# Loading q for two chunks at once, with two tokens per partition, and storing twelve token tiles late

## The chip, the cores and the metric

The kernel runs on one core of a Trainium2 chip. The core has a matrix engine (TensorE, PE), a vector engine (VectorE, DVE), a scalar engine (ScalarE, ACT), a general engine (GpSimd, POOL) and a synchronisation engine (SyncE, SP), and 16 DMA engines that move data between the large memory (HBM) and the on-chip memory (SBUF). The metric is the device time of one execution in microseconds (us); lower is better.

## The reference

There are two stages. The first is a gated linear attention, a recurrence over 768 tokens for 4 x 8 heads of width 48. The second takes its output, 3072 tokens of width 384, through two matrix products with a squared relu between them.

```python
def _attn_ref(q, k, v, alpha):            # each (4, 8, 768, 48), float32
    for t in range(S):
        state = alpha[:, :, t, :, None] * state + np.einsum('bhd,bhe->bhde', k[:, :, t], v[:, :, t])
        y[:, :, t] = np.einsum('bhd,bhde->bhe', q[:, :, t], state)

def _moe_ref(x, w_in, w_out):             # x: y as (3072, 384); w_in (384, 2048); w_out (2048, 384)
    r = np.maximum(x @ w_in, 0.0)
    return (r * r) @ w_out                # (3072, 384), float32
```

## The kernel before

**Tiles.** The 3072 tokens are 24 chunks (or token tiles) of 128 tokens; a batch has six. Each chunk goes through the attention in its chunked form: the logarithm of alpha is summed along the chunk by a matmul with a triangular matrix, exponentials of the sums scale q and k, the scores q·k are masked with the triangle `utri_b` (the `sm` multiplies), and the output is the masked scores times v plus q times the state of the chunks before. The result is turned into `xT_big`, which holds x transposed. Then groups of one, two or four tiles go through the second stage: w_in, relu on ScalarE (`r`), square on DVE (`gT`), w_out, eviction into `ob` or `keep`, and a store of 128 rows of 1536 B.

**Two ways for q and k.** Up to chunk 10, q and k are scaled in token order and turned by TensorE. From chunk `RAW` = 11 on they are "raw": POOL casts them to bf16 (`rawb`), SP issues a DMA transpose for each (`rawt`), and DVE multiplies the turned tiles by exponentials that ScalarE makes from turned sums (`e_qAT`, `e_kiT`, lines 507 and 510).

**Loads.** SP issues one load of 192 KB for each of q, k, v and alpha of a chunk (line 371). Its pieces are 192 B long, since a head's 48 numbers of one token are contiguous. Six buffers for each tensor let loads run up to six chunks ahead. SP works in order: a DMA transpose that waits for a POOL cast holds up the loads behind it. The alpha loads (`at`) feed the logarithm on ScalarE (line 396).

**Order.** A planner (`Plan`) lays out all operations by estimated durations before the program is emitted, and every engine then runs its own list in that order. A gate (`LEAD`) keeps the attention a few chunks ahead of the second stage, and the matmuls of both are interleaved on TensorE.

**Stores.** Tiles 0 to 7 (`HELD` = 8) are kept in SBUF and stored by two SP transfers of four tiles each, planned for 150 us on (line 763). Tiles 8 to 17 are written out as they come: 5 to 17 are given to POOL (`POOL_OUT`), so that POOL issues ten stores (line 772). Tiles 18 to 22 are issued by SP (line 772), and tile 23 by SP in two halves of 192 columns (line 721). `ob` has six buffers. The chunks 18 to 22 are turned into `xT_big` by DMA transposes from SP (line 620), the others by TensorE.

Of the kernel before, what the change touches and what calls it, by code (L numbers as in the profile page):

```python
# [38 lines left out]
class Op:  # L39


    def __init__(self, eng, dur, emit, deps=(), prio=0.0, takes=None, gives=None, lat=None, at=0.0):
        self.eng, self.dur, self.emit = eng, dur, emit
        self.deps = []
        for d in deps:
            if d is not None:
                d = d if isinstance(d, tuple) else (d, None)
                if d[0] is not None:
                    self.deps.append(d)
        self.prio = prio  # L50
        self.takes, self.gives, self.lat, self.at = takes, gives, lat, at
        self.start = self.done = None

# [5 lines left out]
class Plan:  # L59
# [13 lines left out]
    def ready(self, op):  # L73
        t = op.at
        slack = PE_SLACK if "PE" in op.durs else 0.0
        if slack and self.free.get("PE", 0.0) > PE_CALM:
            slack = 0.25
        for d, x in op.deps:
            if d.done is None:
                return None  # L80
            if x is None:
                t = max(t, d.done + (slack if d.eng != "PE" else 0.0))
            else:
                t = max(t, d.start + d.dur + x)
        if op.takes is not None:
            best = None
            for sl in op.takes:
                f = sl.free_at()
                if f is not None and (best is None or f < best):
                    best, op.slot = f, sl  # L90
            if best is None:
                return None
            t = max(t, best)
        return t

    def run(self, gate):
        free = self.free
        while any(self.pending.values()):
# [34 lines left out]
            if op.takes is not None:  # L133
                self.ready(op)
                op.slot.release.append(op.gives if op.gives is not None else op)
            self.order.append(op)
            self.on_pick(op)
# [4 lines left out]
def kernel(  # L142
# [26 lines left out]
    w_out_r = moe_w_out.rearrange("(j p) n -> p j n", p=P)  # L169
    out_r = out.rearrange("(tt p) n -> tt p n", p=P)  # L170

    consts = ctx.enter_context(tc.tile_pool(name="consts", bufs=1))
# [24 lines left out]
    utri_b = consts.tile([P, 1, P], BF16)  # L197
    nc.gpsimd.tensor_copy(utri_b[:, 0, :], utri_f)
    JN, JP = 4, 32
    JW = P + JN - 1  # L200
# [29 lines left out]
    nc.vector.memset(ae_s, 0.0)  # L230
    xT_big = big.tile([P, KT, n_tok], BF16)
    gT_s = big.tile([P, FT, 2 * P], BF16, name="gT2", tag="gT2")
# [78 lines left out]
    EARLY = 4  # L311
    RAW = 11
    XTURN = (18, 23)
    TLD, TLAT, TLATE = 1.0, 4.0, 2.0
    NR = 3
    R = {}

    def raw_tiles():
        if R:
            return  # L320
        R["b"] = stage.tile([P, NR, 2, H, DP], BF16, name="rawb", tag="stage")
        nc.gpsimd.memset(R["b"][:, :, :, :, D:], 0.0)
        R["t"] = stage.tile([P, NR, 2, NP, P], BF16, name="rawt", tag="stage")
        R["i"] = stage.tile([P, 2, NP, P], BF16, name="aiT", tag="stage")

# [38 lines left out]
    def add_load(s, nm):  # L364
        d = C[s]
        b, c = divmod(s, NCH)

        def ld():
            if nm not in d:
                d[nm] = loads.tile([P, H, D], FP32, name=nm)  # L370
            pin(nc.sync.dma_start(out=d[nm], in_=SRC[nm][b, c]))
        prev = C[s - LB].get("use_" + nm) if s >= LB else None
        d["ld_" + nm] = add("DMA", LD if s < 4 else LD1, ld, prev, lat=2.0 if s < 4 else LAG if s < 6 else 2.4, at=0.6)

    def add_chunk(s):
        d = C[s]
        b, c = divmod(s, NCH)
# [30 lines left out]
        if raw:  # L408
            w, wz = s % NR, s % 2

            def e_rb(j, nm):
                raw_tiles()
                pin(nc.gpsimd.tensor_copy(R["b"][:, w, j, :, 0:D], d[nm]))  # L413

            def e_turn(j):
                pin(nc.sync.dma_start_transpose(out=R["t"][:, w, j], in_=R["b"][:, w, j].rearrange("p h d -> p (h d)")))
            rt = []
            for j, nm in enumerate(["qt", "kt"]):
                cb = add("POOL", 0.55, lambda j=j, nm=nm: e_rb(j, nm), d["ld_" + nm],
                         *([C[s - NR]["turn"][j]] if s >= RAW + NR else []), prio=-5.0)  # L420
                d["use_" + nm] = cb
                t_ = add("TR", TLD, lambda j=j: e_turn(j), cb, *([C[s - NR]["turned"][j]] if s >= RAW + NR else []), lat=TLAT)
                t_.late = TLATE
                rt.append(t_)
            d["turn"] = rt
        vb = d["use_vt"] = add("POOL", 0.55, e_vb, d["ld_vt"], old, prio=-5.0)
# [22 lines left out]
        def e_AT():  # L449
            d["qkT"] = work.tile([P, 2 * NP, P], BF16, name="qkT")  # L450
            pin(nc.scalar.activation(d["qkT"][:, NP:2 * NP, :], d["pmT"], AF.Exp))  # L451

# [25 lines left out]
        if raw:  # L478
# [9 lines left out]
            aiT = add("ACT", 0.48, e_AiT, pT, after(aT), *([C[s - 2]["turned"][1]] if s >= RAW + 2 else []), **g)  # L488
            pT.gives = aiT
            if not last:  # L490
                ae0 = add("ACT", 0.18, lambda: e_aeT(0), pT, after(aiT), **g)
# [14 lines left out]
        def e_qAT():  # L506
            pin(nc.vector.tensor_mul(d["qkT"][:, 0:NP, :], R["t"][:, w, 0], d["qkT"][:, NP:2 * NP, :]))

        def e_kiT():
            pin(nc.vector.tensor_mul(d["qkT"][:, NP:2 * NP, :], R["t"][:, w, 1], R["i"][:, wz]))  # L510
        if raw:
            if not last:
                mk = d["use_kt"] = add("DVE", 0.47, e_kI, ai, d["ld_kt"], old, **g)
            cp = add("DVE", 0.34, e_qAT, aT, rt[0], **g)
            cpk = add("DVE", 0.34, e_kiT, aiT, rt[1], cp, **g)
            d["turned"] = [cp, cpk]
        else:
            mq = d["use_qt"] = add("DVE", 0.47, e_qA, a_, d["ld_qt"], old, **g)
            mk = d["use_kt"] = add("DVE", 0.47, e_kI, ai, d["ld_kt"], old, **g)

        def e_p1q():
# [26 lines left out]

        def e_p2():
            sc = d["sc"] = ps_sc.tile([P, 2, NP, P], FP32, name="sc")  # L550
            t = d["qkT"]
            for p in range(NP):
                for hh in range(2):
                    sl = slice(64 * hh, 64 * hh + 64)
                    mm(sc[:, hh, p, :], lhsT=t[sl, NP + p, :], rhs=t[sl, p, :], start=True, stop=True)
        p2 = d["p2"] = plan.add(Op("PE", 0.42, e_p2, [cp, cpk], takes=[sl_sc], lat=0.10, **g))

        def e_sm(hh):
            if hh == 0:
                d["sm"] = work.tile([P, 2, NP, P], BF16, name="sm")  # L560
            pin(nc.vector.tensor_mul(d["sm"][:, hh], d["sc"][:, hh], utri_b.to_broadcast([P, NP, P])))  # L561
        sm0 = add("DVE", 0.6, lambda: e_sm(0), p2, **g)
        sm1 = add("DVE", 0.6, lambda: e_sm(1), p2, after(sm0), **g)
        p2.gives = sm1

        if not last:
# [51 lines left out]
        if XTURN[0] <= s < XTURN[1]:  # L618
            def e_xt():
                pin(nc.sync.dma_start_transpose(out=xT_big[:, :, s * P:(s + 1) * P], in_=d["xn"]))  # L620
            d["x"] = add("TR", 0.8, e_xt, xn, lat=TLAT)
# [5 lines left out]
        def e_xT():  # L627
            cast(xT, xT_big[:, :, s * P:(s + 1) * P], d["px"])
        xT = add({"ACT": 0.36, "DVE": 0.27} if s < EARLY else "DVE", 0.27, e_xT, p4, prio=-9.0)
# [13 lines left out]
    POOL_OUT = (5, 18)  # L643
    HELD, HELD_AT = 8, 150.0
    KEEP, held_ev = {}, []
# [6 lines left out]
    def add_moe1(g, f0, before, lo=0, hi=None, per=1):  # L652
        hi = GN[g] if hi is None else hi
        t0, n = (GT[g] + lo) * P, (hi - lo) * P
        w = per * n
# [35 lines left out]
    def add_last(g, tt, before, pools):  # L691
# [3 lines left out]
        for hf in range(2):  # L695
# [24 lines left out]
            def e_out(box=box, cols=cols):  # L720
                pin(nc.sync.dma_start(out=out_r[t][:, cols], in_=box["ob"]))
            add("OUT", 0.35, e_out, ev, at=0.0)
        return op

    def add_moe2(g, tt, before, box, quarters, pools):
# [22 lines left out]
        def e_ev():  # L748
            if held:
                if t % 4 == 0:  # L750
                    KEEP[t // 4] = stage.tile([P, 4, d_model], FP32, name="keep", tag="stage")
                box["ob"] = KEEP[t // 4][:, t % 4, :]
# [8 lines left out]

        def e_held():
            pin(nc.sync.dma_start(out=out_r[t - 3:t + 1].rearrange("t p n -> p t n"), in_=KEEP[t // 4]))
        if held:
            held_ev.append(ev)
            if t % 4 == 3:
                add("OUT", 2.2, e_held, *held_ev[-4:], at=HELD_AT)
            return op

        def e_out():  # L770
            dma = nc.gpsimd if pool_out else nc.sync
            pin(dma.dma_start(out=out_r[GT[g] + tt], in_=box["ob"]))
        pool_out = POOL_OUT[0] <= GT[g] + tt < POOL_OUT[1]
# [59 lines left out]

    LEAD = 3.7

    def gate(op):
        s = getattr(op, "gla", None)
        if s is not None:
            return s <= LEAD + (prog["m1"] + prog["m2"]) / 5.12
        return True  # L840
# [60 lines left out]
```

## Time and profile before

| | |
|---|---|
| Median of 3 runs | 184.71 us (184.20 to 185.06) |
| Time of the profiled execution | 185.07 us |
| Its span, first to last instruction | 183.4 us |
| PE busy | 177.5 us (97%) |
| DVE, ACT, POOL busy | 127.1, 126.5, 39.4 us |
| Hardware DMA queue (SP's) | 119536 packets, 31.83 MB, 80.7% of 16 engines' span |
| Software DMA queue (POOL's) | 640 packets, 1.97 MB, 3.2% |
| 192 KB loads of q, k, v, alpha: issue to landing | 4.0, 3.6, 3.8, 4.0 us (medians) |
| Stores of 192 KB by SP, halves of 96 KB | 1.9, 1.6 us |

Times in the page and in the views count from the first instruction of the span. The slices cut the span into 40 equal parts; a digit is the busy share in tenths. A row of a timeline has the start, the duration, the engine, the line, the operation, its output and inputs and how often it follows itself; in brackets stands the idle time before it and what ended that. A row of waits has the waiting instruction, the one that ended the wait, the total, the number and the longest. The view of DMA has packets, bytes, the share of 16 engines' time in the stretch asked for, and the issues with their time to landing.

### The profile page before, as it was taken

What the parts mean: (1) busy time and instruction counts of PE and PEld (TensorE: products, weight loads), DVE (VectorE), ACT (ScalarE), POOL (GpSimd) and SP (SyncE); (2) the same over time, 40 slices, a digit from 0 to 9 for tenths busy, and PEclk for the clock granted to TensorE, in tenths of its full rate; (3) what the DMA queues carried; (4) which work ended last, traced back from release to release, by engine and by line L of the source; (5) the groups of instructions that cost most, each with busy time, mean ns of one, the idle gap of its engine ahead of it and who ended that gap; (6) DMA issues with size and microseconds to landing.
All of it is one profiled execution on the core that took longest, in us unless ns stands there. A gap on an engine that the chain in (4) does not pass through costs nothing.

```text
span 183.4 us, 4946 instructions
## 1 busy us (share of the span) xinstructions
PE 177.5 (97%) x1908; PEld 130.5 (71%) x1908; DVE 127.1 (69%) x273; ACT 126.5 (69%) x286; POOL 39.4 (21%) x80
## 2 busy tenths in 40 slices
PE   7999999899999999999999998999999999999993
PEld 2577884567769877867768776667766777778663
DVE  1179898684999998778877867748855984744200
ACT  3677799226859996966967859847975895767321
POOL 8221100021131142132223133342323512000000
PEclk9999999999999999999999999999999999999999
DMA  5999999999999999998999599898898898901022
GB/s 168 215 212 252 302 366 321 326 220 204 177 191 201 194 179 173 141 190 161 150 193 202 113 240 186 161 227 162 170 201 182 176 163 194 301 13 43 12 77 86
DMA packets 120200, 34.12 MB, mean 186 GB/s; under 512 B 112400, under 2 KB 118928, under 8 KB 120176
## 3 DMA queue, kind: packets, MB, share of 16 engines
q1 hardware_dynamic: 119536, 31.83, 80.7%
q0 software_dynamic: 640, 1.97, 3.2%
q8 instruction: 15, 0.25, 0.6%
q14 instruction: 9, 0.07, 0.2%
HBM read 25.17 MB, written 4.72 MB: 163 GB/s over the span
## 4 chain that ended last, share of the span: by engine, by line
PE 49%; DMA 2%; ACT 1%; issue 0%; DVE 0%
PE bank L240 45%; DMA at<-in_alpha_dram 2%; PE sc L240 2%; PE st L240 1%; PE bank L243 1%; ACT aiT L454 0%; ACT r L676 0%; ACT ob L758 0%; ACT L_s L396 0%; ACT ob L716 0%; DVE xT_big L388 0%; ACT qkT L451 0%
## 5 line engine op out<-in xcount | busy, mean ns | idle before, releaser
L240 PE MATMUL bank<-xT_big,w_in_b 128*128 128x256 bf16 (+2 forms) x636 | 76.6, 262 | 0.9 <-ACT r L676 0.7
L240 PE MATMUL bank<-w_out_b,gT 128*128 128x384 bf16 (+1 forms) x400 | 71.6, 320 | 0.5 <-DVE w_out_b L296 0.5
L676 ACT ACTIVATE r<-bank 128x512 bf16<-128x512 f32 x96 | 56.6, 606 | 11.3 <-PE bank L240 9.9
L240 PEld LDWEIGHTS <-w_in_b 128*128 128x128 bf16 x636 | 52.7, 98 | 10.6 <-issue 1.5
L240 PEld LDWEIGHTS <-gT 128*128 128x128 bf16 x416 | 37.2, 98 | 18.7 <-DVE w_out_b L296 1.0
L684 DVE TENSOR_TENSOR gT<-r 128x512 bf16<-128x512 bf16 x96 | 41.8, 453 | 10.2 <-ACT r L676 9.0
L561 DVE TENSOR_TENSOR sm<-sc,utri_b 128x512 bf16<-128x512 f32 x48 | 30.8, 684 | 5.9 <-PE sc L240 5.7
L405 POOL CAST vb<-vt 128x384 bf16<-128x384 f32 x24 | 13.6, 569 | 69.1 <-DMA vt<-in_v_dram 55.2
L386 ACT CAST xn<-bank 128x384 bf16<-128x384 f32 x24 | 11.6, 482 | 11.6 <-PE bank L240 11.5
L505 DVE TENSOR_TENSOR kI_s<-kt,Ainv 128x384 bf16<-128x384 f32 x21 | 12.8, 611 | 7.8 <-ACT Ainv L466 7.8
L240 PEld LDWEIGHTS <-qkT 64*128 64x128 bf16 (+1 forms) x272 | 10.7, 95 | 6.4 <-issue 2.4
L586 ACT CAST sb<-st 128x384 bf16<-128x384 f32 x20 | 9.6, 482 | 7.7 <-DVE st L581 7.5
L758 ACT COPY ob<-bank 128x384 f32<-128x384 f32 x14 | 6.7, 480 | 8.0 <-PE bank L240 8.0
L396 ACT ACTIVATE L_s<-at 128x384 bf16<-128x384 f32 x20 | 10.5, 527 | 2.4 <-DMA at<-in_alpha_dram 2.3
L240 PE MATMUL bank<-warm 128*128 128x256 bf16 (+1 forms) x54 | 10.9, 348 | 1.3 <-DVE warm L188 1.3
L502 DVE TENSOR_TENSOR qA_s<-qt,A 128x384 bf16<-128x384 f32 x11 | 6.3, 575 | 8.0 <-ACT A L462 8.0
L413 POOL CAST rawb<-qt 128x384 bf16<-128x384 f32 x13 | 7.4, 570 | 20.3 <-DMA qt<-in_q_dram 20.3
L413 POOL CAST rawb<-kt 128x384 bf16<-128x384 f32 x13 | 7.6, 587 | 19.0 <-DMA kt<-in_k_dram 11.1
L581 DVE TENSOR_TENSOR st<-st,ae_s 128x384 f32<-128x384 f32 x20 | 11.1, 556 | 0.5 <-PE st L240 0.5
L466 ACT ACTIVATE Ainv<-bank 128x384 bf16<-128x384 f32 x21 | 10.5, 501 | 1.1 <-PE bank L240 1.0
L240 PE MATMUL sc<-qkT 64*128 64x128 bf16 x192 | 9.5, 219 | 0.0
L240 PEld LDWEIGHTS <-sm 128*128 128x128 bf16 x192 | 8.1, 96 | 1.7 <-issue 0.2
(64 smaller groups left out, 165.7 us busy)
## 6 DMA issues: line engine op xcount, KB each, us to landing
qt<-in_q_dram SPq DMA_DIRECT2D x24, 192.0 KB, 4.0
kt<-in_k_dram SPq DMA_DIRECT2D x24, 192.0 KB, 3.6
vt<-in_v_dram SPq DMA_DIRECT2D x24, 192.0 KB, 3.8
at<-in_alpha_dram SPq DMA_DIRECT2D x20, 192.0 KB, 4.0
wo<-in_moe_w_out_dram SPq DMA_DIRECT2D x4, 768.0 KB, 8.5
out_dram<-ob POOLq DMA_DIRECT2D x10, 192.0 KB, 3.1
wi<-in_moe_w_in_dram SPq DMA_DIRECT2D x4, 384.0 KB, 5.3
wi<-in_moe_w_in_dram SPq DMA_DIRECT2D x2, 768.0 KB, 8.3
```

Source lines behind the costliest of these rows:

```text
L240: pin(nc.tensor.matmul(*a, **kw))
L386: pin(nc.scalar.copy(out_t, in_t))
L396: pin(nc.scalar.activation(L[:, :, 0:D], d["at"], AF.Ln))
L405: pin(nc.gpsimd.tensor_copy(d["vb"], d["vt"]))
L413: pin(nc.gpsimd.tensor_copy(R["b"][:, w, j, :, 0:D], d[nm]))
L466: pin(nc.scalar.activation(d["Ai"], d["pm"][:, 0:HD].rearrange("p (h d) -> p h d", h=H), AF.Exp, scale=-1.0))
L505: pin(nc.vector.tensor_mul(kI[:, :, 0:D], d["kt"], d["Ai"]))
L561: pin(nc.vector.tensor_mul(d["sm"][:, hh], d["sc"][:, hh], utri_b.to_broadcast([P, NP, P])))
L581: pin(nc.vector.tensor_mul(st4, st4, bcast(ae, D)))
L586: pin(nc.scalar.copy(d["sbt"], d["st"]))
L676: pin(nc.scalar.activation(box["r"][:, 0:w], box["ph"][:, 0:w], AF.Relu))
L684: pin(nc.vector.tensor_mul(gT[g][:, f0:f0 + per, lo * P:lo * P + n], r, r))
```

## The change

**q in pairs.** `RAW` becomes 10. For the raw chunks, an even chunk and the odd one after it share one load of q of 384 KB (`add_q_pair`): partition p takes the tokens 2p and 2p+1 of 256, so that a piece is 384 B. POOL casts it in two operations and SP turns it in two transposes, one for the even and one for the odd tokens. An even chunk's queries are the first 64 partitions of both, an odd chunk's the last 64. So the queries of a chunk stand in the order of 64 even tokens and then 64 odd ones. The exponential `e_AT` writes in that order, the multiply `e_qAT` reads two blocks of 64, and the mask is `utri_q`, its columns in that order. k, v and alpha stay as they were, one load for each chunk. The rows of x and of the result keep that order up to the store, where `rows(t)` puts them back: the destination is two blocks of 64 rows, each with every second row of the output.

**Late stores.** `HELD` becomes 12: tiles 8 to 11 are kept too, in a tile of their own. Tiles 8 and 9 are stored in one transfer, tiles 10 and 11 in one each.

**Space.** `xT_big` keeps 12 chunks instead of 24 and is written around. q has three pair buffers (`q_s`).

**Prepared but not in use.** Scores of two chunks at a time are written (`DUO`), but its bound of 99 leaves all chunks on the old way.

```diff
+    out_q = out.rearrange("(tt i r) n -> tt r i n", i=DP, r=2)
+    def rows(t):
+        return out_q[t] if t >= RAW else out_r[t]
...
+    utri_q = consts.tile([P, 1, P], BF16)
+    nc.gpsimd.tensor_copy(utri_q[:, 0, :].rearrange("p (r i) -> p r i", r=2), utri_f.rearrange("p (i r) -> p r i", r=2))
...
-    xT_big = big.tile([P, KT, n_tok], BF16)
+    XR = 12
+    xT_big = big.tile([P, KT, XR * P], BF16)
+    q_s = big.tile([P, 3, 2 * HD], FP32)
...
-    RAW = 11
+    RAW = 10
...
+    def add_q_pair(s):
+        b, c = divmod(s, NCH)
+        src = q[b, :, c * P:(c + 2) * P, :].rearrange("h (p r) d -> p h (r d)", r=2)
+        Q = q_s[:, s // 2 % 3, :].rearrange("p (h rd) -> p h rd", h=H)
+        w = s // 2 % 2
+        old = [o for x in (s - LB, s - LB + 1) for o in C[x]["use_q"]]
+        d = C[s]
+        ld = d["ld_qt"] = add("DMA", 1.6, lambda: pin(nc.sync.dma_start(out=Q, in_=src)), *old, lat=2.4, at=0.6)
+        def e_rb(r):
+            raw_tiles()
+            pin(nc.gpsimd.tensor_copy(R["qb"][:, w, r, :, 0:D], Q.rearrange("p h (r d) -> p h r d", r=2)[:, :, r, :]))
+        def e_turn(r):
+            pin(nc.sync.dma_start_transpose(out=R["qt"][:, w, r], in_=R["qb"][:, w, r].rearrange("p h d -> p (h d)")))
...
         def e_AT():
             d["qkT"] = work.tile([P, 2 * NP, P], BF16, name="qkT")
-            pin(nc.scalar.activation(d["qkT"][:, NP:2 * NP, :], d["pmT"], AF.Exp))
+            pin(nc.scalar.activation(d["qkT"][:, NP:2 * NP, :].rearrange("p n (r i) -> p n r i", r=2),
+                                     d["pmT"].rearrange("p n (i r) -> p n r i", r=2), AF.Exp))
...
         def e_qAT():
-            pin(nc.vector.tensor_mul(d["qkT"][:, 0:NP, :], R["t"][:, w, 0], d["qkT"][:, NP:2 * NP, :]))
+            t = R["qt"][:, s // 2 % 2, :, :, s % 2 * 64:(s % 2 + 1) * 64].rearrange("p r n i -> p n r i")
+            m = d["qkT"].rearrange("p n (r i) -> p n r i", r=2)
+            pin(nc.vector.tensor_mul(m[:, 0:NP], t, m[:, NP:2 * NP]))
...
-    HELD, HELD_AT = 8, 150.0
+    HELD, HELD_AT = 12, 150.0
...
-                pin(nc.sync.dma_start(out=out_r[t][:, cols], in_=box["ob"]))
+                pin(nc.sync.dma_start(out=rows(t)[..., cols], in_=box["ob"]))
...
-        def e_held():
-            pin(nc.sync.dma_start(out=out_r[t - 3:t + 1].rearrange("t p n -> p t n"), in_=KEEP[t // 4]))
+        def e_held(lo, n):
+            k = KEEP[lo // 4][:, lo % 4:lo % 4 + n, :]
+            dst = rows(lo) if n == 1 else out_r[lo:lo + n].rearrange("t p n -> p t n")
+            pin(nc.sync.dma_start(out=dst, in_=k[:, 0, :] if n == 1 else k))
...
-            pin(dma.dma_start(out=out_r[GT[g] + tt], in_=box["ob"]))
+            pin(dma.dma_start(out=rows(GT[g] + tt), in_=box["ob"]))
```

In the changed kernel the loads of q pairs have line 415, the casts and transposes of q 419 and 422, those of k 517 and 520, the stores of tiles 12 to 22 line 871, the held ones 857, and the halves of tile 23 line 813.

More of the change, by code (lines that the diff above doesn't have):

```diff
@@ L51, in __init__ @@
         self.takes, self.gives, self.lat, self.at = takes, gives, lat, at
+        self.holds = []
         self.start = self.done = None
@@ L93, in ready @@
             t = max(t, best)
+        for sl, _ in op.holds:
+            f = sl.free_at()
+            if f is None:
+                return None
+            t = max(t, f)
         return t
@@ L135, in run @@
                 op.slot.release.append(op.gives if op.gives is not None else op)
+            for sl, user in op.holds:
+                sl.release.append(user)
             self.order.append(op)
@@ L311 @@
     EARLY = 4
-    RAW = 11
+    RAW = 10
     XTURN = (18, 23)
+    DUO = 99
+    tails = []
     TLD, TLAT, TLATE = 1.0, 4.0, 2.0
@@ L320, in raw_tiles @@
             return
[L321 to L324, printed above, removed]
+        b_ = stage.tile([P, 6, H, DP], BF16, name="rawb", tag="stage")
+        t_ = stage.tile([P, 6, NP, P], BF16, name="rawt", tag="stage")
+        i_ = stage.tile([P, 6, NP, P], BF16, name="aiT", tag="stage")
+        R["qb"] = b_[:, 0:4].rearrange("p (w r) h d -> p w r h d", r=2)
+        R["qt"] = t_[:, 0:4].rearrange("p (w r) n t -> p w r n t", r=2)
+        R["i"] = i_[:, 0:2]
+        R["kt"] = [t_[:, 4], t_[:, 5], i_[:, 2]]
+        R["kb"] = [b_[:, 4], b_[:, 5], i_[:, 3].rearrange("p n (a d) -> p (n a) d", a=2)]
+        R["on"] = True
+        nc.gpsimd.memset(b_[:, :, :, D:], 0.0)
+        nc.gpsimd.memset(R["kb"][2][:, :, D:], 0.0)
     JLD = 1.18
@@ L366, in add_load @@
         b, c = divmod(s, NCH)
+        if nm == "qt" and s >= RAW:
+            if s % 2 == 0:
+                add_q_pair(s)
+            d["ld_qt"] = C[s // 2 * 2]["ld_qt"]
+            return
         def ld():
-            if nm not in d:
+            if nm == "qt":
+                d[nm] = q_s[:, s // 2 % 3, s % 2 * HD:(s % 2 + 1) * HD].rearrange("p (h d) -> p h d", h=H)
+            elif nm not in d:
                 d[nm] = loads.tile([P, H, D], FP32, name=nm)
@@ L373, in add_load @@
         d["ld_" + nm] = add("DMA", LD if s < 4 else LD1, ld, prev, lat=2.0 if s < 4 else LAG if s < 6 else 2.4, at=0.6)
-    def add_chunk(s):
+    def add_q_pair(s):
[11 more added lines that the diff above has]
+            pin(nc.sync.dma_start_transpose(out=R["qt"][:, w, r], in_=R["qb"][:, w, r].rearrange("p h d -> p (h d)")))
+        first = s < RAW + 4
+        d["use_q"], d["qturn"] = [], []
+        for r in range(2):
+            cb = add("POOL", 0.55, lambda r=r: e_rb(r), ld, *([] if first else [C[s - 4]["qturn"][r]]), prio=-5.0)
+            t_ = add("TR", TLD, lambda r=r: e_turn(r), cb, *([] if first else [C[x]["turned"][0] for x in (s - 4, s - 3)]), lat=TLAT)
+            t_.late = TLATE
+            d["use_q"].append(cb)
+            d["qturn"].append(t_)
+        C[s + 1]["use_q"], C[s + 1]["qturn"] = d["use_q"], d["qturn"]
@@ new lines, in add_chunk, with add_scores, dst, e_p2 @@
+    def add_chunk(s):
+        tail = add_head(s)
+        if s < DUO:
+            add_scores(s)
+            tail()
+        elif s % 2 == 0:
+            tails.append(tail)
+        else:
+            add_scores(s - 1, s)
+            tails.pop()()
+            tail()
+    def add_scores(*pair):
+        def dst(s):
+            d = C[s]
+            if len(pair) == 2 and s == pair[0]:
+                d["sc"] = [banks[sl.bank].tile([P, NP, P], FP32, name=f"bank{sl.bank}") for sl in GLA_BANKS]
+            else:
+                t = ps_sc.tile([P, 2, NP, P], FP32, name="sc")
+                d["sc"] = [t[:, hh] for hh in range(2)]
+        def e_p2():
+            for s in pair:
+                dst(s)
+                t = C[s]["qkT"]
+                for p in range(NP):
+                    for hh in range(2):
+                        sl = slice(64 * hh, 64 * hh + 64)
+                        mm(C[s]["sc"][hh][:, p, :], lhsT=t[sl, NP + p, :], rhs=t[sl, p, :], start=True, stop=True)
+        mask = utri_q if pair[0] >= RAW else utri_b
+        def e_sm(d, hh):
+            if hh == 0:
+                d["sm"] = work.tile([P, 2, NP, P], BF16, name="sm")
+            pin(nc.vector.tensor_mul(d["sm"][:, hh], d["sc"][hh], mask.to_broadcast([P, NP, P])))
+        g = dict(prio=-10.0 + pair[0] * 0.01)
+        p2 = plan.add(Op("PE", 0.18 + 0.24 * len(pair), e_p2, [o for s in pair for o in C[s]["cps"]], lat=0.10, **g))
+        for s in pair:
+            d = C[s]
+            d["p2"] = p2
+            sm0 = add("DVE", 0.6, lambda d=d: e_sm(d, 0), p2, prio=-10.0 + s * 0.01)
+            sm1 = add("DVE", 0.6, lambda d=d: e_sm(d, 1), p2, after(sm0), prio=-10.0 + s * 0.01)
+            d["sms"] = [sm0, sm1]
+            p2.holds += [(sl_sc, sm1)] if s == pair[-1] else list(zip(GLA_BANKS, [sm0, sm1]))
@@ L376, in add_chunk, with add_head @@
+    def add_head(s):
         d = C[s]
@@ L409, in add_chunk, with e_rb, e_turn @@
             w, wz = s % NR, s % 2
-            def e_rb(j, nm):
+            def e_rb():
                 raw_tiles()
[L413 to L425, printed above, removed]
+                pin(nc.gpsimd.tensor_copy(R["kb"][w][:, :, 0:D], d["kt"]))
+            def e_turn():
+                pin(nc.sync.dma_start_transpose(out=R["kt"][w], in_=R["kb"][w].rearrange("p h d -> p (h d)")))
+            first = s < RAW + NR
+            cb = d["use_kt"] = add("POOL", 0.55, e_rb, d["ld_kt"], *([] if first else [C[s - NR]["turn"]]), prio=-5.0)
+            d["turn"] = add("TR", TLD, e_turn, cb, *([] if first else [C[s - NR]["turned"][1]]), lat=TLAT)
+            d["turn"].late = TLATE
         vb = d["use_vt"] = add("POOL", 0.55, e_vb, d["ld_vt"], old, prio=-5.0)
@@ L489, in add_chunk @@
             pT.gives = aiT
+            ae1 = None
             if not last:
@@ L506, in e_qAT @@
         def e_qAT():
-            pin(nc.vector.tensor_mul(d["qkT"][:, 0:NP, :], R["t"][:, w, 0], d["qkT"][:, NP:2 * NP, :]))
+            t = R["qt"][:, s // 2 % 2, :, :, s % 2 * 64:(s % 2 + 1) * 64].rearrange("p r n i -> p n r i")
+            m = d["qkT"].rearrange("p n (r i) -> p n r i", r=2)
+            pin(nc.vector.tensor_mul(m[:, 0:NP], t, m[:, NP:2 * NP]))
         def e_kiT():
-            pin(nc.vector.tensor_mul(d["qkT"][:, NP:2 * NP, :], R["t"][:, w, 1], R["i"][:, wz]))
+            pin(nc.vector.tensor_mul(d["qkT"][:, NP:2 * NP, :], R["kt"][w], R["i"][:, wz]))
         if raw:
@@ L513, in add_chunk @@
                 mk = d["use_kt"] = add("DVE", 0.47, e_kI, ai, d["ld_kt"], old, **g)
-            cp = add("DVE", 0.34, e_qAT, aT, rt[0], **g)
-            cpk = add("DVE", 0.34, e_kiT, aiT, rt[1], cp, **g)
+            cp = add("DVE", 0.34, e_qAT, aT, *d["qturn"], **g)
+            cpk = add("DVE", 0.34, e_kiT, aiT, d["turn"], cp, **g)
             d["turned"] = [cp, cpk]
         else:
-            mq = d["use_qt"] = add("DVE", 0.47, e_qA, a_, d["ld_qt"], old, **g)
+            mq = add("DVE", 0.47, e_qA, a_, d["ld_qt"], old, **g)
             mk = d["use_kt"] = add("DVE", 0.47, e_kI, ai, d["ld_kt"], old, **g)
+            d["use_qt"], d["use_q"] = mq, [mq]
         def e_p1q():
@@ L547, in add_chunk, with add_tail @@
             p1q.gives = cp
[L549 to L564, printed above, removed]
+        d["cps"] = [cp, cpk]
+        return lambda: add_tail(s, c, last, d, kI, ae, ae1, mk if not last else None, vb, cp, cast, g)
+    def add_tail(s, c, last, d, kI, ae, ae1, mk, vb, cp, cast, g):
+        sm0, sm1 = d["sms"]
         if not last:
@@ L619, in e_xt @@
             def e_xt():
-                pin(nc.sync.dma_start_transpose(out=xT_big[:, :, s * P:(s + 1) * P], in_=d["xn"]))
+                pin(nc.sync.dma_start_transpose(out=xT_big[:, :, s % XR * P:(s % XR + 1) * P], in_=d["xn"]))
             d["x"] = add("TR", 0.8, e_xt, xn, lat=TLAT)
@@ L627, in e_xT @@
         def e_xT():
-            cast(xT, xT_big[:, :, s * P:(s + 1) * P], d["px"])
+            cast(xT, xT_big[:, :, s % XR * P:(s % XR + 1) * P], d["px"])
         xT = add({"ACT": 0.36, "DVE": 0.27} if s < EARLY else "DVE", 0.27, e_xT, p4, prio=-9.0)
@@ L653, in add_moe1 @@
         hi = GN[g] if hi is None else hi
-        t0, n = (GT[g] + lo) * P, (hi - lo) * P
+        t0, n = (GT[g] + lo) % XR * P, (hi - lo) * P
         w = per * n
@@ L750, in e_ev @@
                 if t % 4 == 0:
-                    KEEP[t // 4] = stage.tile([P, 4, d_model], FP32, name="keep", tag="stage")
+                    KEEP[t // 4] = (stage if t < 8 else big).tile([P, 4, d_model], FP32, name="keep" if t < 8 else f"keep{t}", tag="stage" if t < 8 else f"keep{t}")
                 box["ob"] = KEEP[t // 4][:, t % 4, :]
@@ L766, in add_moe2 @@
             if t % 4 == 3:
-                add("OUT", 2.2, e_held, *held_ev[-4:], at=HELD_AT)
+                n = [x for x in (4, 2, 1) if t - 3 + x <= RAW][0] if t - 3 < RAW else 1
+                lo = t - 3
+                while lo <= t:
+                    m = min(n, 4) if lo < RAW else 1
+                    add("OUT", 0.55 * m, lambda lo=lo, m=m: e_held(lo, m), *held_ev[lo:lo + m], at=HELD_AT)
+                    lo += m
             return op
@@ L834 @@
     LEAD = 3.7
+    DUO_LEAD = 3.7, 3.7
     def gate(op):
@@ L838, in gate @@
         if s is not None:
-            return s <= LEAD + (prog["m1"] + prog["m2"]) / 5.12
+            return s <= (LEAD if s < DUO else DUO_LEAD[s % 2]) + (prog["m1"] + prog["m2"]) / 5.12
         return True
```

## The prediction

> **What bounds the kernel now.** I read the head of the page first, then the chain of waits near the end, then the DMA view of two short stretches of the tail, then the DMA view and the waits of the middle.
>
> ```profile
> span 183.4 us, 4946 instructions
> PE 177.5 (97%) x1908; PEld 130.5 (71%) x1908; DVE 127.1 (69%) x273; ACT 126.5 (69%) x286; POOL 39.4 (21%) x80
> PEclk9999999999999999999999999999999999999999
> DMA  5999999999999999998999599898898898901022
> ```
>
> TensorE works 177.5 of 183.4 us at full clock; the loss is 1.3 us in the first 6 us and 2.9 us after its last matmul, neither touched by the change. The DMA row is the second thing to see: full or nearly so until about 160 us, almost empty in the last 20 us.
>
> ```profile
> 169.94 10.56 PE bank L240 x81
> 180.50 0.02 issue
> 180.52 0.32 ACT ob L716
> ```
>
> The chain ends in matmuls, one eviction at 180.52, and a store. So after the last matmul only that one store is exposed. How a store uses the DMA engines is seen where it runs alone, from 168 to 170 us (one 192 KB store) and from 181 to 183 us (the last half store):
>
> ```profile
> DMA packets 144, 0.20 MB, mean 98 GB/s; under 512 B 16, under 2 KB 144, under 8 KB 144
> q1 hardware_dynamic: 144, 0.20, 26.4%
> out_dram<-ob SPq DMA_DIRECT2D x1, 192.0 KB, 1.9
> ...
> DMA packets 144, 0.10 MB, mean 49 GB/s; under 512 B 16, under 2 KB 144, under 8 KB 144
> q1 hardware_dynamic: 144, 0.10, 14.8%
> ```
>
> 128 rows of data and 16 small packets, one for each engine: these stores are dealt over all 16. The full one takes 26.4% of 16 engines over 2 us, 8.45 us of engine time (0.53 us on each); the half 14.8%, 4.74 us. The next lines are of the middle, 120 to 153 us, with seven POOL stores, of which six take nearly all of the software queue's 10.2%:
>
> ```profile
> q0 software_dynamic: 384, 1.18, 10.2%
> ACT L_s L396 <- DMA at<-in_alpha_dram: 1.2, 2, 0.7
> 109.42 0.52 ACT L396 ACTIVATE L_s<-at 128x384 bf16<-128x384 f32 x1 [0.71 <-DMA at<-in_alpha_dram]
> 111.84 0.49 PE L240 MATMUL bank<-xT_big,w_in_b 128*128 128x256 bf16 x3 [0.66 <-ACT r L676]
> ```
>
> Packets of 1.18 MB are six stores: 10.2% of 33 us of 16 engines is 53.9 us, 9.0 us of engine time for each store beside other traffic. The last three lines show the weak place: ScalarE waits for an `at` load, relu behind it is late, and TensorE stands 0.66 us. It is TensorE's only stall over 0.1 us after 60 us.
>
> **The change part by part.** The profiled execution took 185.07 us, 1.67 over its span; the median of the three runs is 184.71, 0.2% lower. Sums are against 185.07.
>
> *Chunk 10 becomes raw.* TensorE loses eight transposes and four one-column matmuls and gains four 128x128 ones. On the chain three transposes take 0.17 us; with the same 0.055 us for the others, the net is about -0.4 us on the path. ScalarE trades one A (0.49) for two exponentials (0.61, 0.63) and DVE a multiply and a copy (0.58, 0.69) for two multiplies (0.46, 0.44): beside TensorE, with over 11 us of idle ahead of the relus. The stride-2 read of PSUM in the exponential of 14 chunks and the split token order in 14 multiplies cost between nothing and twice their time (8.6 and 6.4 us); I take nothing, as element counts are unchanged, and both engines are idle 31% of the span. If that cover were gone, a relu or a score would be late by at most 0.6 us per chunk.
>
> *q in pairs.* From 56 to 66 us 10441 packets, all under 512 B, take 100.7% of 16 engines: 15.4 ns for each 192 B piece. Fourteen loads of 1024 pieces are 13.8 us on every engine. Seven pair loads have as many pieces each, at a price between 15.4 ns and that of the half store's 768 B rows (4.74 us by 128, 37 ns); by bytes about 23, so 10.3 us. Saved 3.5, between 6.9 and -2.8. Two more transposes (of the raw chunk 10) cost about 0.8 us each: what loads leave of the queue's 85.4% between 66 and 153 us, by 512 packets. SP issues seven fewer loads. Of the pair's two casts POOL does the same work as before, but SP has two transposes in a row to wait for; the waits of DVE for a turned tile are ended by ScalarE in every case, never by the transpose, so a microsecond there is covered.
>
> *Four tiles more stored late.* Tiles 8 to 11 leave the middle: four POOL issues and 4 x 0.53 us on every engine. Together the DMA engines have about 4 us less to do before 150 us. TensorE can win from that only its one stall, 0.66 us.
>
> *Stores in token order.* From tile 10 on, the listing of the changed program shows the store's destination as 2x64x384 where before it was 128x384; SBUF's side still has 128 partitions in front. No transfer of the trace has a leading count other than 128, so the cost has to be bounded. If it is still dealt over 16 engines, 0.53 us each. If an engine's share has to be a block of the leading count on both sides, there are only two shares: 64 rows on each of two engines, 8.45/2 = 4.2 us alone, 9.0/2 = 4.5 us in the middle, and 4.74/2 = 2.4 us for a half. I take two, since the leading count is the one thing on which all 16-way transfers of the trace agree. [...]
>
> *The tail with two engines.* SP's stores share one queue; I take it that they land on the same two engines. Behind the transpose of chunk 22, which landed 5.2 us after its issue at 155.12 (160.3), come tiles 8 and 9 on 16 engines (1.1 us, to 161.4), then 10, 11, 18 to 22: seven by 4.2 is 29.4 us, and two halves, 4.7. That fills the two engines without a gap (tile 18 is issued at 159.15, 19 at 167.96, each earlier than the queue reaches it) to 195.5. Before, the half's packets ended at about 182.1 and the span at 183.4; the same 1.3 us gives 196.8, and with 1.67 it is 198.5. TensorE's own end no longer counts; what counts is when the queue starts, and that follows TensorE through chunk 22. No eviction waits for it: six output buffers lie between.
>
> *The middle with two engines.* Tiles 12 to 17 leave by POOL at 123.6, 132.2, 137.6, 139.7, 146.3 and 152.9. On two engines each occupies them for 4.5 us, where it took 0.56 of every one: a load that crosses is late by up to 3.9 us. The transposes have cover, as said. `at` has none: the last one is issued at 132.80, beside the second of these stores, and is read at 136.4, on landing. I put one such delay on the path, 3.9 us; bounds are none and all five stores ahead of 152 us.
>
> Sum: 198.5 - 0.4 - 0.66 + 3.9 = 201.3, rounded 201.
>
> **The rivals.** *Two engines, middle covered.* The 4 us that the DMA engines save arrive before the stores do, and `at` is early enough: 197.4. For it: all four waits of ScalarE for `at` in the span are 2.3 us together, the longest 0.7. Against: 3.9 us is more than all of these. Chance 0.25.
>
> *Every store goes into the load loop.* SP waits in order for casts, so a late load stops the loads behind it: 5 x 3.9 less 4.2 us saved and about 3.4 us that the last turned k lies ready (issue 150.4, landing 3.4 later, read at 157.2), 11.9 us on TensorE: 209.3. For it: the full DMA row. Against: the row has eights after 130 us, so the queue catches up a little between stores. Chance 0.15.
>
> *Other pairs for other stores.* Then nothing queues: the last half starts at about 181.8, takes 2.4, and ends the span 2.1 us later than now; with the middle as forecast 185.1 + 2.1 + 2.8 = 190. Nothing in the trace speaks for it. Chance 0.08.
>
> *Still 16 engines, faster.* The tail is as before, the 0.66 us stall at 111 us and 0.4 us of matmuls go: 184.0, faster by 0.6%. It decides from the point where a store's 64 rows need not stay on one engine, and would be read from 16 small packets per store. Chance 0.10.
>
> **How the numbers follow.** My forecast has 0.42. The range 193 to 209 holds it, the covered middle (down to 4.2 us less, should one late store go out ahead of that transpose) and most of the serial case; outside lie the last two rivals, 0.18, and a little above. A difference of 0.5% is about what can be told here, the three runs being spread over 0.47%. Faster 0.06 and same 0.04 come from the last rival, which lies at that bound; slower 0.90.
>
> **What would show it.** In the changed profile: a store alone with two small packets, landing 4 to 5 us after issue, later ones 10 us and more; the DMA row at 1 in the last slices where all else is 0; the chain ending in a long DMA step behind L813; loads of 6 to 8 us to landing between 124 and 153 us, and ScalarE waiting for `at` by over 3 us. It is wrong if late stores land in 2 us, or if TensorE's last matmul comes before 180 us and the end within 4 us of it.

## The result, and the profile after

The changed kernel took 213.97 us (median of 6 runs, 209.74 to 214.94) against 184.88 us (6 runs, 184.2 to 186.25) for the kernel before. The ratio, 1.140 with a 95% interval of 1.128 to 1.152, counts only the runs within 1.5% of the fastest of their kernel (209.74 and 212.24 us of the change), so the profiled run and the loss of 29 us read from it lie some 3 us above what the ratio says. The profiled execution took 214.03 us, 28.96 more than that of before. It is slower, as forecast, and 5 us past the upper end of the range.

The head of the page comes first: busy times, then TensorE, its granted clock and the DMA engines in 40 slices of 5.3 us.

```profile
span 212.3 us, 4898 instructions
...
PE 181.5 (85%) x1900; PEld 131.9 (62%) x1900; DVE 127.2 (60%) x272; ACT 128.0 (60%) x288; POOL 39.2 (18%) x80
...
PE   7897899999999999999999997595489999999100
...
PEclk9999999999999999999999999579958999999955
DMA  6998999999989688987969695799994697111110
```

There are two places to see. The DMA row ends in five 1s and a 0, the slices after 180 us, and TensorE is done before the last of them. And in the middle, between about 125 and 165 us, TensorE has gaps and its clock falls below full twice, where before it was full throughout. The chain of waits near its end says when TensorE is done:

```profile
145.19 9.67 DMA xT_big<-xn
...
154.90 7.38 PE bank L256 x37
...
178.88 18.29 PE bank L256 x144
197.17 0.02 issue
197.20 0.32 ACT ob L808
```

The last matmul ends at 197.17 us, where it was 180.50: 16.7 us later. From there to the end of the span it is 15.1 us, where it was 2.9: 12.2 us more. Together 28.9 us, the whole loss. So there are two halves to explain. The second is read from the DMA view of 180 to 184 us, where only a store is under way:

```profile
DMA packets 135, 0.20 MB, mean 51 GB/s; under 512 B 3, under 2 KB 135, under 8 KB 135
q1 hardware_dynamic: 135, 0.20, 13.6%
```

In these 4 us some 132 rows are moved with 3 small packets, where before 128 rows brought 16 of them. The queue fills 13.6% of 16 engines all the time: two engines are 12.5%. The first half of the loss stands in the waits of TensorE (us in total, times, longest) and in the time line of SyncE's queue (start, duration):

```profile
PE bank L256 <- ACT r L768: 3.7, 1, 3.7
PE bank L256 <- DMA xT_big<-xn: 3.6, 1, 3.6
PE sc L256 <- DVE qkT L613: 3.2, 2, 2.7
```

```profile
124.81 0.97 SPq L404 DMA_DIRECT2D vt<-in_v_dram  x1
125.87 1.18 SPq L404 DMA_DIRECT2D at<-in_alpha_dram  x1
127.09 4.98 SPq L404 DMA_DIRECT2D kt<-in_k_dram  x1
132.18 2.83 SPq L422 DMA_TRANSPOSE rawt<-rawb  x2
135.07 0.57 SPq L404 DMA_DIRECT2D vt<-in_v_dram  x1
```

The loads issued at 123.56, 124.19 and 135.07 us took SyncE 0.57 us each. Here one issue lasts 4.98 us, until 132.07; GpSimd's store issued at 124.56 landed 8.0 us later. Near the end of that issue, from 130.5 to 131.5 us, the store takes 10.7% of 16 engines and SyncE's queue 4.3%, so most engines are idle while the issue goes on. Everything behind this load, two transposes, a load of v and more, starts some 4.4 us late. The load of alpha ahead of it, issued at 125.87, is late as well, and so is the next one, issued at 139.65. ScalarE waits for both (the first row is the total of the span):

```profile
ACT L_s L500 <- DMA at<-in_alpha_dram: 8.4, 5, 4.0
133.94 0.52 ACT L500 ACTIVATE L_s<-at 128x384 bf16<-128x384 f32 x1 [3.99 <-DMA at<-in_alpha_dram]
145.64 0.52 ACT L500 ACTIVATE L_s<-at 128x384 bf16<-128x384 f32 x1 [2.36 <-DMA at<-in_alpha_dram]
```

Right behind the first of these waits ScalarE makes the relu (`r`) that ends TensorE's wait of 3.7 us. Behind the second it makes the exponentials that DVE needs for the `qkT` that ends TensorE's wait of 2.7 us. The third wait of TensorE, 3.6 us, is for a turned activation: SyncE issued its transpose at 145.19, and it landed 9.67 us later. So a late `at` stands behind two of the three long waits, and a late transpose behind the third. The six stores of GpSimd took this long:

```profile
DMA to landing us min/median/max: 7.2/7.8/9.3
```

Before, GpSimd's ten stores had 2.2, 3.1 and 4.5 us there. Last, the clock behind two of the waits, from the view by stretches (length, busy time of PE, PEld, DVE, ACT and POOL with counts, PEclk, DMA share, GB/s):

```profile
134.00:138.00 4.00, 3.00 (x15) 2.07 (x15) 2.47 (x6) 3.30 (x8) 1.30 (x2) 0.50 0.71 138
154.00:158.00 4.00, 3.10 (x17) 2.20 (x17) 0.98 (x2) 1.33 (x3) 0.00 (x0) 0.51 1.58 111
```

After it has stood for 3.7 us (131.3 to 135.0) and again for 3.6 us (151.3 to 154.9), TensorE works at half its clock (0.50 and 0.51); after the wait of 2.7 us (146.2 to 148.9) it does not: from 149 to 152 us the clock is 1.00. The profile's sum of busy time shows the price: 181.5 us against 177.5, for eight matmuls fewer.

### The profile page after: what moved, and what is told of

It reads as the page before. It is cut to its first block, busy times and chain, and to the rows that moved or that the text cites. A ratio compares the mean times of both kernels' runs of the same rounds, so it can differ in the third digit from the quotient of the medians.

```text
span 212.3 us, 4898 instructions
## 1 busy us (share of the span) xinstructions
PE 181.5 (85%) x1900; PEld 131.9 (62%) x1900; DVE 127.2 (60%) x272; ACT 128.0 (60%) x288; POOL 39.2 (18%) x80
## 5 line engine op out<-in xcount | busy, mean ns | idle before, releaser
L256 PE MATMUL bank<-xT_big,w_in_b 128*128 128x256 bf16 (+2 forms) x636 | 79.9, 271 | 9.1 <-ACT r L768 3.7
L256 PE MATMUL bank<-w_out_b,gT 128*128 128x384 bf16 (+1 forms) x400 | 72.8, 323 | 0.5 <-DVE w_out_b L312 0.5
L256 PEld LDWEIGHTS <-w_in_b 128*128 128x128 bf16 x636 | 54.6, 100 | 20.8 <-issue 8.4
L776 DVE TENSOR_TENSOR gT<-r 128x512 bf16<-128x512 bf16 x96 | 41.4, 453 | 17.5 <-ACT r L768 16.5
L509 POOL CAST vb<-vt 128x384 bf16<-128x384 f32 x24 | 14.1, 591 | 72.2 <-DMA vt<-in_v_dram 60.0
L468 DVE TENSOR_TENSOR sm<-sc,utri_q 128x512 bf16<-128x512 f32 x28 | 18.0, 683 | 4.0 <-PE sc L256 4.0
L606 DVE TENSOR_TENSOR kI_s<-kt,Ainv 128x384 bf16<-128x384 f32 x21 | 12.7, 603 | 12.5 <-ACT Ainv L566 12.5
L490 ACT CAST xn<-bank 128x384 bf16<-128x384 f32 x24 | 11.6, 484 | 10.1 <-PE bank L256 10.1
L256 PEld LDWEIGHTS <-qkT 64*128 64x128 bf16 (+1 forms) x272 | 10.7, 96 | 10.1 <-DVE qkT L613 4.8
L468 DVE TENSOR_TENSOR sm<-sc,utri_b 128x512 bf16<-128x512 f32 x20 | 12.8, 682 | 1.0 <-PE sc L256 0.8
L419 POOL CAST rawb<-q_s 128x384 bf16<-128x384 f32 x14 | 6.9, 521 | 22.6 <-DMA q_s<-in_q_dram 22.6
L603 DVE TENSOR_TENSOR qA_s<-q_s,A 128x384 bf16<-128x384 f32 x10 | 5.8, 579 | 8.3 <-ACT A L562 7.5
L256 PE MATMUL bank<-warm 128*128 128x256 bf16 (+1 forms) x54 | 9.6, 316 | 1.3 <-DVE warm L200 1.3
L610 DVE TENSOR_TENSOR qkT<-rawt,qkT 128x512 bf16<-128x512 bf16 x14 | 5.9, 420 | 6.4 <-ACT qkT L550 6.0
```

The lines of the kernel that those rows point to most:

```text
L256: pin(nc.tensor.matmul(*a, **kw))
L419: pin(nc.gpsimd.tensor_copy(R["qb"][:, w, r, :, 0:D], Q.rearrange("p h (r d) -> p h r d", r=2)[:, :, r, :]))
L468: pin(nc.vector.tensor_mul(d["sm"][:, hh], d["sc"][hh], mask.to_broadcast([P, NP, P])))
L490: pin(nc.scalar.copy(out_t, in_t))
L509: pin(nc.gpsimd.tensor_copy(d["vb"], d["vt"]))
L606: pin(nc.vector.tensor_mul(kI[:, :, 0:D], d["kt"], d["Ai"]))
```

## The experiments

**The stores, mended one kind at a time.** Three kernels keep the changed kernel and issue a two-block store as two stores of 64 rows each, each with 64 in front on both sides: all of them, only SyncE's, or only GpSimd's. The lines shown are from the first; the two others have `False` for the stores that stay in two blocks.

```
+    def put(dma, t, src, cols=slice(None), two=True):
+        if two and t >= RAW:
+            for r in range(2):
+                pin(dma.dma_start(out=out_q[t][r][:, cols], in_=src[DP * r:DP * (r + 1)]))
+        else:
+            pin(dma.dma_start(out=rows(t)[..., cols], in_=src))
...
-            pin(dma.dma_start(out=rows(GT[g] + tt), in_=box["ob"]))
+            put(dma, t, box["ob"], two=True if pool_out else True)
```

All split:

> The changed kernel, with each of its two-block stores (tiles 10 to 23) issued as two stores of 64 rows, the even and the odd rows of the output: the same bytes to the same places, but 64 in front on both sides. Theory A (a store with two blocks in front goes out on two DMA engines, and this makes the whole loss): tail as in the kernel before, end 3 us after the last matmul, no long stall of TensorE; 184 to 185 us, a stretch with one such store alone shows 16 small packets for each half. Rival B (the middle is lost to the q pairs and their paired transposes on SP, the stores cost the tail alone): TensorE ends near 197 us still, and the time is 200 to 202. Rival C (the number of DMA engines does not matter, the stepped rows of the output do): unchanged at 210 to 215.

Measured: 189.2 us (6 runs, 187.71 to 191.61) against 184.84, ratio 1.022 (1.015 to 1.028). The last matmul ends at 184.78 us, 3.9 us before the end of the span. Of the loss of 29 us, 4.4 are left, so the time lies between the ranges of theory A and rival B. The stepped rows of the output (rival C) are still there, so they are not what costs the 25 us that went.

SyncE's split, GpSimd's six left in two blocks:

> The changed kernel with SP's stores (tiles 10, 11, 18 to 23) issued as two of 64 rows; POOL's six stay two-block. Theory A: TensorE's last matmul still near 197 us, the end 3 us behind it: 200 to 203 us. If POOL's stores do not matter to the middle (rival B too): the same 200 to 203, so that this run alone does not tell A from B; it gives the tail's price, 11 to 13 us.

Measured: 201.13 us (2 runs), ratio 1.088 (1.079 to 1.096). The last matmul ends at 196.05 us, 3.9 us before the end. Its waits of TensorE are those of the changed kernel once more:

```profile
PE bank L263 <- DMA xT_big<-xn: 3.9, 2, 3.6
PE bank L263 <- ACT r L775: 3.6, 1, 3.6
PE sc L263 <- DVE qkT L620: 3.6, 3, 2.6
```

GpSimd's split, SyncE's left in two blocks:

> The changed kernel with POOL's six stores (tiles 12 to 17) issued as two of 64 rows; SP's stay two-block. Theory A: no long stall in the middle, last matmul near 180 us, then SP's queue on two engines from about 161 us for 34 us: 196 to 199 us. Rival B: last matmul near 197, 212 to 215 us.

Measured: 199.9 us (2 runs), ratio 1.081 (1.072 to 1.090), 0.9 us over theory A's range. The middle is not all free: one wait of TensorE of 2.4 us stays, and the last matmul ends at 185.42 us, not near 180. The rest is tail: 13.8 us, in which the DMA row is at 1 until its last slice.

```profile
PE   7899989999999999989999999949999999999200
...
DMA  5999999999899779797778888878985592111110
```

So the six stores of GpSimd cost 11.9 us in the middle (201.13 - 189.2) and those of SyncE 10.7 us behind TensorE (199.9 - 189.2), and the two add up: 189.2 + 11.9 + 10.7 = 211.8 us, which lies among the six runs of the changed kernel (209.74 to 214.94).

**The two-block store alone, in the kernel before.** Nothing of the change but the destination of tiles 12 to 23; their rows land in another order within the tile.

```
+    out_q = out.rearrange("(tt i r) n -> tt r i n", i=DP, r=2)
+    def rows(t):
+        return out_q[t] if t >= 12 else out_r[t]
...
-            pin(dma.dma_start(out=out_r[GT[g] + tt], in_=box["ob"]))
+            pin(dma.dma_start(out=rows(GT[g] + tt), in_=box["ob"]))
```

> The kernel before with two-block destinations for the stores of tiles 12 to 23 (six by POOL, the rest by SP), nothing else; left out is the row order: rows of these tiles land in other places of the same tile. If the two-block store alone makes the loss, whatever q does: POOL's six cost 10 to 13 us of TensorE, SP's queue from about 160 us on holds five whole and two half stores, 25.7 us, so that it hardly fills before the end of TensorE: 205 to 210 us. If the loss needs q in pairs: under 195.

Measured: 205.75 us (2 runs), ratio 1.118 (1.113 to 1.124), inside the range of the first theory. One line of access pattern, with the same bytes and as many stores, makes the greater part of the loss by itself. Both halves are there: the waits of TensorE, and 12.2 us behind its last matmul at 191.7.

```profile
PE bank L244 <- DMA xT_big<-xn: 7.5, 2, 5.1
```

**All but the two-block stores.** The changed kernel with every store back in one block; the rows stay in the pair's order.

```
     def rows(t):
-        return out_q[t] if t >= RAW else out_r[t]
+        return out_r[t]
```

> The changed kernel with plain stores of 128 consecutive rows for every tile: q in pairs, raw from chunk 10, twelve tiles late, all as changed; left out is the return to token order, so rows within the tiles from 10 on stay in the order of even and then odd tokens. Theory A: 184 to 185 us, at most 0.5 us below the kernel before by its one stall and 0.4 us of matmuls. Rival B: 200 to 202. Rival C: 184 to 185 too. If it is below the run with split stores, the difference is the price of twice as many store issues (0.3 to 0.6 us).

Measured: 187.69 us (6 runs), ratio 1.018 (1.012 to 1.023), 2.7 us over theory A's range. The rest of the change is no gain but a loss of 1.8%. TensorE has three waits of about 1 us between 129 and 144 us. The next kernels look for what makes them.

**Chunk 10 raw, alone** (`RAW = 10` in the kernel before):

> The kernel before with chunk 10 raw as well (RAW = 10), nothing else. If the 3 to 4 us that remain with split or plain stores came from one more raw chunk (two more transposes on SP, more exponentials on ScalarE): 187 to 188 us. If they come from the pairing of q: 184 to 185 us, 0.4 us of matmuls being all that it can save.

Measured: 184.3 against 184.14 us (12 runs), ratio 1.0007 (0.9985 to 1.0029): nothing.

**Twelve tiles stored late, alone** (in the kernel before `HELD = 12`, and the twelve-tile ring for `xT_big` that makes room for them):

> The kernel before with twelve tiles stored late instead of eight (128 consecutive rows each; xT kept for 12 chunks to make room, as in the change), nothing else. By the prediction's term the DMA engines lose 2.1 us of work in the middle and TensorE at most its stall: 184.0 to 185. If late stores cost the rest: 187 to 188.

Measured: 184.79 us (12 runs), ratio 1.004 (1.002 to 1.006): a small cost, not a gain. What is left of the 1.8 to 2.2% is then the pair of q, if the parts add up.

**`at` a chunk earlier.** In the kernel with all stores split the chain goes through a load of `at` (`125.20 5.51`), as the forecast had it. This kernel loads `at` two chunks ahead instead of one.

```
-                if nm == "at" and 9 <= d < NT - 1:
-                    add_load(d + 1, nm)
+                if nm == "at" and d >= 9:
+                    for x in ((10, 11) if d == 9 else (d + 2,)):
+                        if x < NT:
+                            add_load(x, nm)
```

> The changed kernel with split stores and each alpha load from chunk 11 on put one chunk earlier in the order of loads, nothing else. If what remains is ScalarE's wait for alpha behind a run of five loads and a run of transposes that the pairing makes: 185 to 186.5 us against 189.2 with split stores alone, and ScalarE's wait for alpha near 0. If the remaining loss is in q, k or v: 188 to 190 us, with alpha's wait gone all the same.

Measured: 187.42 us (6 runs), ratio 1.022 (1.017 to 1.026), as without it; 187.42 is in neither range. From 120 to 146 us ScalarE no longer waits for `at`, but TensorE now waits for a turned activation:

```profile
PE bank L263 <- DMA xT_big<-xn: 1.7, 1, 1.7
```

So `at` alone does not make what is left: with it out of the way, another transfer of SyncE's queue is late.

**The pair a chunk earlier.** All stores split, and the pair's load and everything that hangs on it is put in front of the odd chunk ahead of it.

```
-            if s % 2 == 0:
-                add_q_pair(s)
+            for x in ([10] if s == 10 else [s + 1] if s % 2 and s + 1 < NT else []):
+                add_q_pair(x)
```

> As the kernel with all two-block stores issued in two halves (189.2 us, 2.2% over before), but each load of two chunks of q is issued one chunk earlier, at the odd chunk in front of its pair. SyncE's queue then holds at most three or four loads in a row with a transpose between, where it had five loads and then two transposes of q. Theory A, the rest of the loss is the bunching of loads and transposes on SyncE's queue: 184 to 186.5 us, TensorE without waits of over 1 us after 120 us. Theory B, the rest comes from the paired layout itself (384-byte pieces, strided reads, token order): 188 to 190 us, unchanged. I lean to A.

Measured: 186.13 us (12 runs), ratio 1.009 (1.006 to 1.011), inside the range of theory A. TensorE's waits after 60 us are down to one:

```profile
PE sc L263 <- DVE qkT L620: 0.5, 1, 0.5
```

The paired layout is all still there, so its strided reads and wider pieces are not what cost the time in the middle. The last matmul ends at 180.05 us, 0.45 ahead of the kernel before. Behind it are 3.9 us instead of 2.9; there the two halves of the last tile now leave as four stores that SyncE issues one after the other (its fourteen split stores take 0.47 to 0.6 us to issue, 0.54 in the median).

**q of two chunks in a row, without the pair.** The kernel before, with the loads, casts and transposes of q of chunks 12 and 13, 14 and 15 and so on placed next to each other.

```
+            load1(s, nm)
+            load1(s + 1, nm)
+            add_q_turn(s)
+            add_q_turn(s + 1)
```

> The kernel before with its packets, layout and stores unchanged, but from chunk 12 on the loads, casts and transposes of q of two chunks follow one another, as the pair's do in the changed kernel. Theory A (bunching on SyncE's queue): 186.5 to 189 us, with a wait of TensorE of 0.8 to 2 us behind a late load or transpose after 120 us. Theory B (the paired layout): 184 to 185 us, as before.

Measured: 185.11 us (12 runs), ratio 1.003 (0.9995 to 1.007). TensorE's waits after 60 us are two, 1.0 us together, the longest 0.5. Theory A missed here: a row of loads in SyncE's queue is not enough in itself. The order that the scheduler made of it was also not the pair's order, a transpose of k and two loads stood between the loads and the transposes of q, so it doesn't tell which neighbour does the harm.

**Activations turned by TensorE.** All stores split, and `XTURN = (18, 18)`:

> As the kernel with all two-block stores issued in two halves (189.2 us), but the activations of chunks 18 to 22 are turned by TensorE and copied by VectorE, not by a transposing DMA: five transposes of 1.2 us of issue leave SyncE's queue, TensorE gains 15 transposes of about 0.055 us, 0.8 us. Theory A, a late turned tile is what TensorE waits for and SyncE's queue makes it late: 186 to 188 us. Theory B (the paired layout): 189.5 to 190.5 us, the old loss and the 0.8 us.

Measured: 188.24 us (6 runs), ratio 1.018 (1.014 to 1.023), in neither range. The interval overlaps that of the kernel with these transposes (1.015 to 1.028). If TensorE's 0.8 us is taken off, they could account for some 1.4 of the 4.4 us, an estimate that this run is too coarse to show; they are not the whole.

**Two queues for the last tile.** The kernel with the pair a chunk earlier, the last tile's second blocks issued by ScalarE:

> As the kernel with split stores and the pair loaded one chunk earlier (186.1 us, 0.9% over before, TensorE done at 180.05 us and 4.0 us after that), but of the two halves of the last tile the second 64-row blocks are issued by ScalarE's queue beside SyncE's. If what is left of the loss lies in the four issues of 0.55 to 0.6 us that follow one another on SyncE: 0.6 us less, 185.0 to 185.6 us, 3.4 us after the last matmul, 0.3 to 0.6% over before. If it lies in the middle: unchanged. A version that beats the kernel before by over 0.5% is expected by neither.

Measured: 186.57 against 185.18 us (12 runs), ratio 1.007 (1.004 to 1.011). The time misses the range of 185.0 to 185.6, and the ratio can't be told from 1.009. In the profiled execution TensorE is busy for 2 tenths of the last slice of 4.65 us, so some 3.3 to 3.7 us lie behind the last matmul, between the 3.9 of one queue and the 2.9 of before. No version of the change beat the kernel before.

## Why the prediction was wrong in size

**Two engines: right.** The one thing that no trace showed, how a store with 2x64 rows is dealt, came out as taken: 13.6% of 16 engines and 51 GB/s from 180 to 184 us, where one store alone had 26.4% and 98 GB/s over 2 us before.

**The tail: right.** The forecast laid seven stores of 4.2 us and two halves of 2.4 us behind chunk 22's transpose, 34.1 us, and 1.3 us to the end. Counted back from the end of the span, 212.3 - 1.3 - 34.1 = 176.9 us: 5.0 us after that transpose was issued, at 171.92, where the forecast had 6.3. That transpose itself was 16.8 us later than in the kernel before, exactly as TensorE was (16.7). The kernel with only SyncE's stores in two blocks has the tail by itself.

**The middle: the step that failed.** "I put one such delay on the path, 3.9 us." The profile of the changed kernel shows 16.7 us there, in three terms. Three waits of 3.7, 2.7 and 3.6 us make 10.1. The half clock behind them makes 4.0 (busy time 181.5 against 177.5). The first 30 us have 2.5 us more idle time (4.1 against 1.6 us); two kernels with split stores that differ only in the last tile's stores have 5.0 and 1.6 us there in their profiles, so it is not counted to the change. The one delay of the forecast is there as it was told: ScalarE waits 3.99 us for `at`, and TensorE 3.7 us behind it. What failed is that it was to be the only one. A second wait for `at`, 2.36 us, stands behind TensorE's second wait, and the third is for a turned activation, of a kind of which the forecast said "The transposes have cover, as said."

The forecast let each load that a store crosses be late by one store's 3.9 us. The profile shows that SyncE's issue stops as well (4.98 us instead of 0.57), and that all behind it in the queue starts late, the transposes too. Why the issue stops is not shown: no view has the engines one by one. In the kernel before with two-block stores both of TensorE's long waits (5.1 and 2.4 us) are for turned activations, none for a relu. ScalarE's longest wait for `at` at its logarithm (`L_s`) is 0.7 us in the kernel before, 2.7 us with the pair and GpSimd's stores split, and 3.9 us with the pair and only SyncE's stores split. So the 3.99 us fit the store and the pair's place together.

The rival "Every store goes into the load loop" had 0.15 and a price of 11.9 us. The three waits less the one they replaced (10.1 - 0.66) come near it, but not by its sum of five times 3.9 us less slack, so the nearness is in part luck; at 209.3 us it lacked the clock.

**The clock: a term left out.** The trace of before had full clock everywhere and, after 60 us, no wait of TensorE over 0.66 us, so it could not show what a long one costs. In the changed kernel the clock was 0.50 and 0.51 behind the waits of 3.7 and 3.6 us and 1.00 behind that of 2.7 us. Other runs differ: with all stores split it was 0.72 in the mean of 132 to 138 us, behind a wait of 2.0 us that ended at 131.8, and 1.00 in the 6 us ahead of these and behind them; with GpSimd's stores split it was at 7 tenths in the slice from 134.5 to 139.4 us, behind a wait of 2.4 us that ended at 133.9. So a wait of 2 us can cost the clock, and its length alone does not decide. By the 4.0 us of busy time behind two waits, the forecast should have carried some 2 us more for each wait near 4 us.

**The pair of q: wrong sign.** The DMA time was forecast well: 384-byte pieces took 26.0 ns in the mean of the changed kernel's packets, where 23 was taken and 192-byte pieces cost 16.5 (15.8 before). But no TensorE time came of it, and SyncE's new order cost what the forecast called covered. The turned q is not on the path in the kernel with all stores split: from 103.3 us on its chain has two DMA steps, the load of `at` at 125.20 (5.51 us) and a turned activation at 139.67 (5.70 us). Placed a chunk earlier, the pair leaves TensorE a single wait of 0.5 us in the middle of its profile, and the ratio falls from 1.022 to 1.009, which shows its place to be the cause of about 1.3 of the 2.2%. Which neighbour in the queue does it stays open: neither a row of q loads, nor `at`, nor the turned activations alone explains it. Of the 0.9% left, about 1 us is seen behind the last matmul; the rest stays open too.

**Small terms.** Chunk 10 as a raw chunk was priced at -0.4 us, which is -0.2%, and measured 0.07% (-0.15 to 0.29%). Four more late stores were priced as a gain of up to 0.66 us, together with the pair, and cost 0.4% alone. That the strided reads cost nothing was right: the exponential took 610 ns (612 before), the multiply 420 ns (461 before).

## What to carry to other kernels

Before a store is given another row order, look at the leading count of both sides of its access pattern: here a store of 2x64 rows took 13.6% of 16 DMA engines, about the share of two, where one of 128 rows alone had over nine tenths of them at its peak (before, 168 to 170 us), and a split into two stores of 64 rows took most of the loss away (24.8 of 29 us). Here GpSimd's stores, 7.2 to 9.3 us to landing instead of 2.2 to 4.5, delayed not only what crossed them but the issue of later transfers on SyncE's queue (4.98 us instead of 0.57), so price the queue, not the single late tile. And let a forecast wait of TensorE of 2 us or more carry the lost clock as a possible term: it came behind waits of 2.0 to 3.7 us here, though not behind all.

## What was not expected of the hardware

SyncE's issue of a plain load, 0.57 us at 124.19, lasted 4.98 us while GpSimd's two-block store was under way. The 26 stores of 64 rows from `ob` landed 2.8 us after their issue in the median (the pair a chunk earlier), where the 15 of 128 rows from `ob` had taken 2.5 us before. The split adds an issue of 0.47 to 0.6 us on SyncE for each tile (the same run); in the time of the kernel it can't be seen, as split and plain stores (1.022 and 1.018) have overlapping intervals. TensorE's clock fell behind a wait of only 2.0 us (all stores split, 0.72 in the mean of 132 to 138 us).
